# Seven products in place of eight in both halves of a feed-forward layer, with its row sums made on the chip from split rows

## The chip, the core and the metric

The kernel runs on one core of a Trainium2 chip. The metric is device time in microseconds (us). The kernel before took 1064.24 us (median of three runs, 1063.29 to 1064.33).

A core has five engines, each with a queue of its own that it works through in order: TensorE (PE; its weight loads are shown as PEld), VectorE (DVE), ScalarE (ACT), GpSimd (POOL) and SyncE (SP). SP computes nothing here; it issues most of the DMA transfers. POOL and ACT issue a few as well.

## The reference

All arrays are float32. S is 2048 rows, D is 576 columns, DFF is 4608.

```python
xn = layernorm(A_q)                                   # 2048 x 576, no scale or bias
k_shift = short causal convolution of A_k with shift_k (4 taps, per column)
kv = k_shift * A_v
y = long causal convolution of kv with ssm_k (2048 taps, per column, by FFT) + kv * ssm_D
out = A_q + xn * y + relu(xn @ B_w1) @ B_w2           # w1: 576 x 4608, w2: 4608 x 576
```

There are two independent pieces: the feed-forward layer (the two matrix products with the relu) and the long convolution, which the kernel does as a transform by matrix products. They meet in the last sum.

## The kernel before

**The arithmetic.** TensorE works on rounded float32, so each operand of the feed-forward layer is split into a high and a low part, and each product is three matmuls: high by high, high by low, low by high. A high part is made by an ACT copy, the low one by a subtraction: on POOL for weights (`split_lo`, line 428), on DVE for rows and for the hidden layer.

**The tiling.** The 2048 rows form four blocks of 512. The first half of the program works on two blocks, the second half on the other two. DFF is cut into 18 chunks of 256 columns (`NPAIR`), and both halves go through all 18. The program counts chunks 0 to 35: 0 to 17 in the first half, 18 to 35 in the second. A *visit* is one chunk with one block; there are 72, and each chunk is visited twice in a row, once with each block (`visits`, line 1125). In what follows "visit 8" is the ninth, which is the first with chunk 4.

**The first product, plain.** `mm1` (line 557) makes 128 hidden columns for 512 rows: 14 matmuls of 512 columns, 12 over four slices of 128 of D and two over the remaining 64, whose high and low part are stacked. A visit has two of them, 28 matmuls of 512. The rows are the transposed blocks `b1` and `b2` (slices 0, 2 and 1, 3) and `xr` (the remaining 64), each with high and low part.

**The first product by seven products.** `quad` (line 585) treats a visit as a 2 x 2 by 2 x 2 block product and makes seven products where eight would be plain. It needs sums of weight blocks (`sum_w` on POOL, line 486) and sums of row blocks: `t1`, which stands in the second half of `b1` in place of the plain rows, and `t2` to `t4` in a tile `t`. Each of the seven is six matmuls of 256 columns; the 64 remaining rows of D are added by four matmuls of 512. Between the products ACT copies two partial sums of 256 columns (lines 592, 593) and DVE adds two (597, 600). Before the change the whole first half uses `mm1` and the whole second half uses `quad`.

**The second product.** `unit` (line 612) takes 128 rows and 288 output columns through one or two chunks, six matmuls of 288 columns a chunk, and DVE adds the result to an accumulator (lines 634, 638). Units are queued by `phase` and taken by `fill` after each quarter of a visit, two units of one chunk or one of two chunks at a time.

**The convolution stream.** `conv` is a Python generator with four stages: `fk` (transform of the taps), `fx` (short convolution on DVE and transform of the rows), `fm` (product in the frequency domain) and `fo` (back transform, gate, sum). Each `yield` ends a step. `tick` (line 1077) counts the columns of feed-forward matmuls issued and takes the next step when a rate allows it; the rate comes from `SHARE`, the part of the feed-forward columns at which the stream is to end. A negative yield is a pause. The constants of `fk` and `fx` come by DMAs that POOL issues (`load_const`, line 665), three buffers deep. The instructions of each engine are finally ordered by a scheduler that goes by program order and by when it expects an operand to be ready.

**The rows of the second half.** `later_xT` (line 301) is a generator that makes, during the first half, the transposed and split rows of the blocks of the second half, with the row sums: it loads a block's four row tiles in two transfers of two tiles at a time, normalizes, stores them, loads them back in 32 x 32 blocks, turns them on DVE, sums and splits, and stores `b1` (with `t1` in it), `b2`, `t` and `xr` to DRAM (`kept`). Two tiles of 3072 floats a partition hold its work; they are those of `t`, which the first half does not use otherwise. `fetch` (line 415) loads everything back between the halves.

**Weights.** A chunk of `w1` lands in `both_w1`: in the first half alternately in its two halves of five slices; with the seven products one half takes the raw weights, the other the sums. A chunk of `w2` lands in two halves with a buffer each (tag `r2`, line 446), and the next load is queued right behind the split (`later_w2`). `opening` lists what the first visits do; `split_next` says when the weights of the next chunk are split.

## Time and profile before

| | us |
|---|---|
| median of three runs | 1064.24 |
| profiled execution, its own time | 1066.44 |
| profiled execution, span of the trace | 1064.6 |
| PE busy | 1051.3 |
| DVE busy | 740.6 |
| ACT busy | 550.9 |
| POOL busy | 399.1 |

The profiled execution took 1.84 us more than the span of its trace, and 2.2 us more than the median. Matmuls are pipelined: one of 288 columns is shown with 295 ns, though the next one starts 133 ns later. So the time of a matmul is read here from start to start in a row of them, not from its own duration. In the trace the first half's products carry the name `psh`, the second half's `psa` and `psb`; `pso` is the second product and `psf` the convolution.

### The profile page before, as it was taken

The page shows a single profiled execution, that of the slowest core. Times are in us where ns is not written, and L with a number is a line of the kernel's source. Part 1 is how long each engine was busy: PE and PEld are TensorE (multiplying, and loading weights), DVE is VectorE, ACT ScalarE, POOL GpSimd, SP SyncE. Part 2 cuts the span into 40 slices and gives each one's busy share as a digit, 9 for nine tenths or more (in the row PEclk, how much of TensorE's full clock was granted, in tenths as well). Part 3 has the DMA queues.
Part 4 walks back from the last instruction along what each step waited for, and adds up shares of the span by engine and source line. Part 5 has one row for each costly group of instructions (what it writes and reads, how often), then busy time and mean ns, then how long its engine had stood idle before and what let it go on. Part 6 is the DMA issues. An engine that isn't in the chain of part 4 may idle for free.

```text
span 1064.6 us, 19975 instructions
## 1 busy us (share of the span) xinstructions
PE 1051.3 (99%) x7153; PEld 989.4 (93%) x7153; DVE 740.6 (70%) x1312; ACT 550.9 (52%) x1201; POOL 399.1 (37%) x398
## 2 busy tenths in 40 slices
PE   8999999999999999999999999999999999999998
PEld 5889999998899999999999999999999999999997
DVE  4539778787776887752477788778787763666664
ACT  5226556434433434432467877777877753344341
POOL 4133333333133223342334334435244444444641
PEclk9999999999999999999999999999999999999999
DMA  9944867788656667754896566556556557667854
GB/s 229 204 100 133 227 174 203 207 242 228 192 157 185 161 177 221 237 160 165 275 264 193 157 181 181 174 182 188 160 154 204 166 168 219 213 206 228 276 183 111
DMA packets 156302, 204.44 MB, mean 192 GB/s; under 512 B 32845, under 2 KB 122703, under 8 KB 155180
## 3 DMA queue, kind: packets, MB, share of 16 engines
q1 hardware_dynamic: 143308, 189.00, 60.2%
q0 software_dynamic: 12576, 13.44, 5.6%
q8 instruction: 56, 0.92, 0.4%
q10 hardware_dynamic: 320, 0.74, 0.3%
q14 instruction: 42, 0.34, 0.1%
HBM read 133.92 MB, written 55.05 MB: 178 GB/s over the span
## 4 chain that ended last, share of the span: by engine, by line
PE 93%; DMA 3%; DVE 2%; ACT 1%; issue 1%; POOL 0%; SPq 0%; ACTq 0%; DVEq 0%
PE pso L629 41%; PE psh L566 21%; PE psb L542 13%; PE psf L904 7%; PE psa L542 6%; PE psf L684 3%; DMA acc<-in_x 1%; PE psf L1048 1%; PE psf L1050 1%; DMA both_w<-in_w 1%; DMA both<-in_v 1%; DMA xs<-both 0%; DVE both L821 0%; ACT hh L548 0%; DVE k L969 0%
## 5 line engine op out<-in xcount | busy, mean ns | idle before, releaser
L629 PE MATMUL pso<-w,hh 128*128 128x288 f32 x2304 | 469.2, 295 | 1.6 <-ACT w L528 0.8
L629 PEld LDWEIGHTS pso<-w,hh 128*128 128x128 f32 x2304 | 372.5, 188 | 9.0 <-ACT w L528 1.2
L629 PE MATMUL pso<-w,ll 128*128 128x288 f32 x1152 | 330.0, 295 | 0.0
L428 POOL TENSOR_TENSOR g<-both_w,g 128x256 fp32r<-128x256 f32 (+2 forms) x145 | 167.8, 1163 | 348.7 <-ACT g L466 294.4
L566 PE MATMUL psh<-b,g 128*128 128x512 f32 x864 | 218.7, 396 | 0.5 <-ACT b L223 0.2
L629 PEld LDWEIGHTS pso<-w,ll 128*128 128x128 f32 x1152 | 213.6, 188 | 1.0
L566 PEld LDWEIGHTS psh<-b,g 128*128 128x128 f32 x864 | 157.9, 189 | 31.1 <-DVE b L224 0.5
L638 DVE TENSOR_TENSOR acc<-pso,acc 128x288 f32<-128x288 f32 x232 | 101.8, 450 | 60.7 <-PE pso L629 59.1
L428 POOL TENSOR_TENSOR w<-r,w 128x576 fp32r<-128x576 f32 x72 | 113.8, 1580 | 57.4 <-ACT w L528 57.4
L548 ACT ACTIVATE hh<-psh 128x512 fp32r<-128x512 f32 x72 | 42.9, 597 | 148.6 <-PE psh L566 148.4
L549 DVE SCALAR_TENSOR_TENSOR ll<-psh,hh 128x512 fp32r<-128x512 f32 x72 | 49.3, 686 | 71.9 <-ACT hh L548 71.5
L542 PE MATMUL psb<-t,g 128*128 128x256 f32 x648 | 97.5, 281 | 0.3 <-DVE psa L597 0.3
L542 PEld LDWEIGHTS psb<-t,g 128*128 128x128 f32 x648 | 86.2, 188 | 2.4 <-DVE psb L600 1.1
L466 ACT ACTIVATE g<-both_w 128x256 fp32r<-128x256 f32 (+2 forms) x145 | 76.2, 542 | 10.7 <-PE psb L542 8.7
L495 POOL TENSOR_TENSOR both_w<-both_w 128x256 f32<-128x256 f32 x72 | 63.6, 902 | 28.9 <-DMA both_w<-in_w 27.5
L542 PE MATMUL psa<-b,g 128*128 128x256 f32 x432 | 63.3, 280 | 0.0
L542 PE MATMUL psb<-b,g 128*128 128x256 f32 x432 | 58.1, 281 | 0.0
L548 ACT ACTIVATE hh<-psa 128x512 fp32r<-128x512 f32 x36 | 21.5, 598 | 70.0 <-PE psa L542 69.8
L542 PEld LDWEIGHTS psa<-b,g 128*128 128x128 f32 x432 | 56.7, 188 | 0.0
L542 PEld LDWEIGHTS psb<-b,g 128*128 128x128 f32 x432 | 54.6, 188 | 0.0
L670 POOL DMA_DIRECT2D wx<-in_fwd x32 | 17.6, 549 | 98.5 <-PE psf L684 91.4
L634 DVE SCALAR_TENSOR_TENSOR acc<-pso,rstd,acc 128x288 f32<-128x288 f32 x72 | 36.5, 511 | 19.2 <-PE pso L629 18.5
(134 smaller groups left out, 1688.1 us busy)
## 6 DMA issues: line engine op xcount, KB each, us to landing
r<-in_w SPq DMA_DIRECT2D x72, 288.0 KB, 3.7
zy<-vo SPq DMA_DIRECT2D x64, 288.0 KB, 3.1
zo<-zy SPq DMA_DIRECT2D x32, 576.0 KB, 4.0
both_w<-in_w SPq DMA_DIRECT2D x35, 512.0 KB, 4.4
zk<-zk SPq DMA_DIRECT2D x64, 144.0 KB, 2.6
ztk<-zk SPq DMA_DIRECT2D x32, 288.0 KB, 3.3
ztx<-zx SPq DMA_DIRECT2D x32, 288.0 KB, 3.1
k<-k SPq DMA_DIRECT2D x64, 144.0 KB, 2.6
```

The lines of the kernel that those rows point to most:

```text
L428: return nc.gpsimd.tensor_tensor(dst, src, hi, OP.subtract)
L466: nc.scalar.activation(hi, src, AF.Copy)
L495: nc.gpsimd.tensor_tensor(dst, a, b, op)
L542: done["pe"] = nc.tensor.matmul(ps, a, m, start=start and i == 0, stop=i == len(seq) - 1, skip_group_check=not start)
L548: done["act"] = nc.scalar.activation(hh, ps, AF.Relu)
L549: lows.append(nc.vector.scalar_tensor_tensor(ll, ps, 0.0, hh, op0=OP.max, op1=OP.subtract))
L566: done["pe"] = nc.tensor.matmul(ps, a, m, start=i == 0, stop=i == len(seq) - 1)
L629: done["pe"] = nc.tensor.matmul(ps[:, :NH], a, m, start=c == 0, stop=c == len(seq) - 1)
L634: done["acc"] = nc.vector.scalar_tensor_tensor(acc[t][:, dc], ps[:, :NH], rstd[:, t:t + 1], acc[t][:, dc], op0=OP.mult, op1=OP.add)
L638: done["acc"] = nc.vector.tensor_tensor(acc[t][:, dc], ps[:, :NH], acc[t][:, dc], OP.add)
L684: nc.tensor.matmul(ps[:, :NH], w[:, n, :], stk, start=n == 0, stop=n == 1)
L904: nc.tensor.matmul(ps[:, :NH], a, m[:, cols], start=n == 0, stop=n == 2)
```

## The change

- `PLAIN = (4, 3)`: the first product is plain only for the first four chunks of the first half and the first three of the second. The other 14 and 15 chunks go by `quad`.
- `later_xT` no longer sums. It keeps plain split rows, and works in one row buffer of 576 floats (`spare`): one row tile at a time is loaded, normalized and stored, and pieces of 256 rows are loaded back, turned, split and stored. Its steps are taken after every quarter of a visit.
- `block_sums` makes `t2` to `t4` for a block on the chip from the split rows, in eight steps of DVE and ACT work, during the plain visits (visits 4 to 7, and 37 to 41). `first_sum` then writes `t1` over the second half of `b1`, when the last plain visit of that block is done: for one block at the end of visit 7 (41), for the other at the start of visit 8 (42), with two extra `fill()` behind it. `t` is neither stored to DRAM nor fetched.
- `w1` has one raw buffer from chunk 2 on. `w2` has one buffer in chunks 2 to 17, since the other one is the row buffer; `next_w2` queues its load a quarter of a visit later than before.
- The constants of `fk` have two buffers in place of three; the turned taps have two of their own in place of one shared with `quad`.
- `split_next` and `opening` follow: plain or summed weights by what the next chunk is.
- `SHARE` is 0.944 in place of 0.97, and a pause of the stream drops what credit it had.

The diff, cut to its core ("..." where lines are left out):

```diff
--- before.py
+++ after.py
@@ -33,6 +33,7 @@
 HALVES = 2
 HB = NB // HALVES
 HT = T // HALVES
+PLAIN = (4, 3)
-SHARE = 0.97
+SHARE = 0.944
-FFN_TOTAL = NPAIR * HB * (W_PLAIN + W_QUAD + 2 * 4 * W_UNIT)
-N_FLOATS = {"b1": 2048, "b2": 2048, "t": 3072, "xr": 512}
+FFN_TOTAL = HB * (sum(PLAIN) * W_PLAIN + (2 * NPAIR - sum(PLAIN)) * W_QUAD
+                  + 2 * NPAIR * 4 * W_UNIT)
+N_FLOATS = {"b1": 2048, "b2": 2048, "xr": 512}
+N_SUMS = 3072
...
-    nrm = dram.tile([HB, P, BT, D], F32, name="nrm")
+    nrm = dram.tile([HB, BT // 2, P, 2, D], F32, name="nrm")
...
-        hold, area = scratch(0, f"rows{b}"), scratch(1, f"area{b}")
...
+        row = spare
+        raw, out_ = row[:, :HR], row[:, HR:2 * HR]
+        both = row[:, :2 * HR].rearrange("p (m n) -> p m n", m=2)
+        for i in range(BT):
+            t = b * BT + i
+            move(row, x, t)
             yield
             yield
             with here():
+                stats(t, row)
+                inv_std(t, 1)
             yield
             with here():
+                normalized(row, row, t)
+            nc.sync.dma_start(nrm[s, i // 2, :, i % 2], row)
+            yield
+        for c in range(5):
+            n = min(P, D - c * P)
+            for r in range(2):
+                rows = slice(r * HR, (r + 1) * HR)
+                src = nrm[s, r].rearrange("(e r) i d -> r i e d", e=4)
+                to = raw[:n].rearrange("p (i e d) -> p i e d", e=4, d=Q)
+                for q in range(n // Q):
+                    nc.sync.dma_start(to[q * Q:(q + 1) * Q],
+                                      src[..., c * P + q * Q:c * P + (q + 1) * Q])
+                yield
+                yield
+                hi = raw[:n].bitcast(F32R)
+                with here():
+                    nc.vector.transpose(out_[:n], raw[:n])
+                    nc.scalar.activation(hi, out_[:n], AF.Copy)
+                yield
+                with here():
+                    nc.vector.tensor_tensor(out_[:n].bitcast(F32R), out_[:n], hi, OP.subtract)
+                if c < 4:
+                    kept_ = kept["b2" if c % 2 else "b1"][s].rearrange("p (m k n) -> p m k n",
+                                                                      m=2, k=2)
+                    nc.sync.dma_start(kept_[:, :, c // 2, rows], both)
+                else:
+                    for m in range(2):
+                        nc.sync.dma_start(kept["xr"][s][64 * m:64 * m + 64, rows], both[:64, m])
+                yield
+
+    def block_sums(s):
+
+        b1, b2 = f32(ops[s, "b1"]), f32(ops[s, "b2"])
+        t = operand(s, "t")
+        tt = nc.vector.tensor_tensor
+        v, w = sum_v, xp.tile([P, NH], F32, tag="m5", name=f"sum{s}", bufs=1)[:, :HR]
+
+        def both(b, kp, r):
+            return [b[:, m, kp, r * HR:(r + 1) * HR] for m in range(2)]
+
+        def high(i, kp, src):
+            nc.scalar.activation(t[:, i, 0, kp], src, AF.Copy)
+
+        def low(i, kp, src):
+            tt(t[:, i, 1, kp], src, t[:, i, 0, kp], OP.subtract)
+
+        for kp in range(2):
+            (h11, l11), (h12, l12) = (both(b1, kp, r) for r in range(2))
+            (h21, l21), (h22, l22) = (both(b2, kp, r) for r in range(2))
+            with here():
+                tt(v, h22, h12, OP.subtract)
+                tt(v, v, l22, OP.add)
+                tt(v, v, l12, OP.subtract)
+                high(1, kp, v)
...
+    def first_sum(s):
+
+        b1 = ops[s, "b1"]
+        tt = nc.vector.tensor_tensor
+        w = xp.tile([P, NH], F32, tag="m5", name=f"first{s}", bufs=1)[:, :HR]
+        for kp, v in enumerate((sum_v, w)):
+            (h11, l11), (h12, l12) = ([f32(b1)[:, m, kp, r * HR:(r + 1) * HR] for m in range(2)]
+                                      for r in range(2))
+            tt(v, h12, h11, OP.subtract)
+            tt(v, v, l12, OP.add)
+            tt(v, v, l11, OP.subtract)
+            nc.scalar.activation(b1[:, 0, kp, HR:], v, AF.Copy)
+        for kp, v in enumerate((sum_v, w)):
+            tt(b1[:, 1, kp, HR:], v, b1[:, 0, kp, HR:], OP.subtract)
...
-                t = t.rearrange("p a b c -> p (a b c)" if name != "t"
-                                else "p k a b c -> p (k a b c)")
+                t = t.rearrange("p a b c -> p (a b c)")
             nc.sync.dma_start(f32(t), kept[name][s])
...
     both_w1 = wp.tile([P, 10, FC], F32, name="both_w1", bufs=1)
+    raw_w2 = wp.tile([P, FT * NH], F32, name="raw_w2", bufs=1)
+    spare = wp.tile([P, FT * NH], F32, name="spare", bufs=1)
+    sum_v = both_w1[:, 9]
+
+    def plain(n):
+        return n % NPAIR < PLAIN[n // NPAIR]
 
     def load_w1(n):
         f0 = (n % NPAIR) * FC
-        r1 = both_w1[:, 5:] if n < NPAIR and n % 2 else both_w1
+        r1 = both_w1[:, 5:] if n == 1 else both_w1
...
     def load_w2(n, h):
         f0 = (n % NPAIR) * FC
-        r2 = wp.tile([P, FT, NH], F32, tag="r2", name=f"r2_{n}_{h}", bufs=2)
+        r2 = spare if h and not 2 <= n < NPAIR else raw_w2
+        r2 = r2.rearrange("p (j d) -> p j d", j=FT)
         nc.sync.dma_start(r2, w2[f0:f0 + FC, h * NH:(h + 1) * NH]
                           .rearrange("(j p) d -> p j d", p=P))
         raw_w[n, h] = r2
...
-    def load_const(pool, src, name, late=False):
-        w = pool.tile([P, 2, P], F32R, tag="wt", name=name, bufs=3)
+    def load_const(pool, src, name, bufs=3, late=False):
+        w = pool.tile([P, 2, P], F32R, tag="wt", name=name, bufs=bufs)
...
                 ws = {}
-                for n in range(3):
-                    ws[n] = load_const(fp, fwd[n // U][:, n % U], f"wk{n}", late=True)
+                for n in range(2):
+                    ws[n] = load_const(fp, fwd[n // U][:, n % U], f"wk{n}", 2, late=True)
...
-                    pool, tag = (xp, "m5") if i % 2 else (fp, "tr")
-                    tr = turned_[i] = pool.tile([P, NH], F32, tag=tag, name=f"tr{t2}", bufs=1)
+                    tr = turned_[i] = fp.tile([P, NH], F32, tag="tr", name=f"tr{t2}", bufs=2)
...
-                    if n + 3 < len(order):
-                        ws[n + 3] = load_const(fp, fwd[(n + 3) // U][:, (n + 3) % U], f"wk{n + 3}")
+                    if n + 2 < len(order):
+                        ws[n + 2] = load_const(fp, fwd[(n + 2) // U][:, (n + 2) % U],
+                                               f"wk{n + 2}", 2)
...
         if c < 0:
             clock["until"] = clock["ffn"] - c
+            clock["conv"] = min(clock["conv"], 0.0)
         else:
             clock["conv"] -= c
...
+    def next_w2(n, h):
+        if n == 0 or NPAIR <= n < HALVES * NPAIR - 1:
             load_w2(n + 1, h)
-
-    opening = {(0, 1): [(later_w2, 0, 0)], (0, 3): [(later_w2, 0, 1)],
-               (1, 1): [(later_w2, 1, 0)], (1, 2): [(load_w1, 2), (load_w1, 3)], (1, 3): [(later_w2, 1, 1)],
+        elif n < NPAIR - 1 or n == NPAIR - 1 and not h:
+            if not h and n > 1:
+                load_w2(n, 1)
+            elif (n == 1) != bool(h):
+                load_w2(n + 1, 0)
+        elif n == NPAIR - 1:
+            for h_ in range(2):
+                load_w2(n + 1, h_)
...
+    def all_sums(q):
+        return (step_ for q_ in (q, q + 1) for step_ in block_sums(visits[q_][1]))
+
+    lasts = [2 * (half * NPAIR + PLAIN[half] - 1) for half in range(HALVES)]
+    begins = [4, 2 * NPAIR + 1]
+    sums_ = [all_sums(q) for q in lasts]
...
-        parts = quad(n, s, q % 2) if half else None
+        if q - 2 in lasts:
+            first_sum(s)
+            fill()
+            fill()
+        parts = None if plain(n) else quad(n, s, q % 2)
...
-            if half:
+                if st == 2 and n > 2:
+                    next_w2(n, second)
+            if not plain(n):
                 tick(W_STAGE[st])
-            if q > 3 and (st % 2 or st == 2 and q % 2):
+            if begins[half] <= q <= lasts[half] + 1:
+                next(sums_[half], None)
+            if q - 1 == lasts[half] and st == 3:
+                for _ in sums_[half]:
+                    pass
+                first_sum(visits[q - 1][1])
+            if q > 3:
                 next(ahead, None)
             fill()
         if m == NPAIR - 1 and not half:
...
-            fetch(s, ("t",))
```

More of the change, by code (lines that the diff above doesn't have):

```diff
@@ L367, in later_xT @@
-        for c in range(2):
-            for q in (0, 2):
-                load(c, (q, q + 1))
-                yield
-        yield
-        for kp in range(2):
-            hi, lo = (b2[:, m].bitcast(F32R) for m in range(2))
-            with here():
-                e0 = turn_over(2 * kp)
-            b11, b12 = e0[:, r12[0]], e0[:, r12[1]]
+        row = spare
[4 more added lines that the diff above has]
+            move(row, x, t)
+            yield
@@ L1131, in split_next @@
     def split_next(n, second, st):
-        if n + 1 < NPAIR:
+        if n + 1 == HALVES * NPAIR:
+            return
+        if plain(n + 1) and plain(n):
             if not second:
@@ L1140, in split_next @@
                 split_rest(n + 1)
-                if n + 3 <= NPAIR:
-                    load_w1(n + 3)
-        elif n + 1 == NPAIR:
+                load_w1(n + 2)
+        elif plain(n + 1):
+            if second:
+                if st < 2:
+                    split_plain(n + 1, st)
+                elif st == 2:
+                    split_rest(n + 1)
+                else:
+                    load_w1(n + 2)
+        elif plain(n):
             if not second:
@@ L1153, in split_next @@
                 load_w1(n + 2)
-        elif n + 1 < HALVES * NPAIR:
-            if second:
-                split_group(n + 1, st)
-                if st == 3 and n + 2 < HALVES * NPAIR:
-                    load_w1(n + 2)
-            else:
-                sum_w(n + 1, st)
+        elif second:
+            split_group(n + 1, st)
+            if st == 3 and n + 2 < HALVES * NPAIR:
+                load_w1(n + 2)
+        else:
+            sum_w(n + 1, st)
     def later_w2(n, h):
@@ L1196, in h3_ffn_kernel @@
                     later_w2(n, second)
-            if half:
+                if st == 2 and n > 2:
+                    next_w2(n, second)
+            if not plain(n):
                 tick(W_STAGE[st])
-            if q > 3 and (st % 2 or st == 2 and q % 2):
+            if begins[half] <= q <= lasts[half] + 1:
[5 more added lines that the diff above has]
+            if q > 3:
                 next(ahead, None)
```

102 lines of the change are left out of this document (17 added, 85 removed).

## The prediction

> **What bounds the kernel now.** I read the page first, then the table of windows, then the timeline of PE.
>
> ```profile
> span 1064.6 us, 19975 instructions
> ...
> PE 1051.3 (99%) x7153; PEld 989.4 (93%) x7153; DVE 740.6 (70%) x1312; ACT 550.9 (52%) x1201; POOL 399.1 (37%) x398
> ```
>
> PE is busy in 1051.3 of 1064.6 us. Since matmuls overlap, "busy" does not yet say that it works at its best pace. The windows say more (time, busy time and instruction count of each engine, granted clock, DMA share, GB/s):
>
> ```profile
> core 0: us, PE busy (x) PEld busy (x) DVE busy (x) ACT busy (x) POOL busy (x), PEclk, DMA share, GB/s
> 240.00:280.00 40.00, 36.37 (x210) 32.69 (x209) 32.07 (x48) 17.82 (x36) 10.69 (x12) 0.96 0.80 215
> 280.00:500.00 220.00, 220.00 (x1320) 199.88 (x1320) 151.45 (x243) 84.62 (x170) 68.29 (x66) 1.00 0.63 183
> 560.00:700.00 140.00, 139.26 (x1055) 136.23 (x1055) 109.26 (x190) 104.37 (x233) 57.20 (x48) 1.00 0.60 176
> 700.00:850.00 150.00, 149.98 (x1147) 147.83 (x1146) 117.89 (x202) 113.75 (x255) 65.64 (x55) 1.00 0.58 175
> ```
>
> In both halves (280 to 500 plain, 560 to 850 with seven products) PE has no idle time to speak of, at the full granted clock. DVE is at 69% in the first and 78% in the others. Only 240 to 280 stands out: PE idle for 3.6 us, and the clock at 0.96 of full. Outside that place a change moves the time if it moves the number or the length of the matmuls. So I need their spacing, from the timeline of PE (start, duration, what, count), first a plain product, then pieces of a seven-product visit:
>
> ```profile
> 386.79 2.95 PE L566 MATMUL psh<-b,g 128*128 128x512 f32 x12
> 389.58 0.63 PE L566 MATMUL psh<-xr,g 128*128 128x512 f32 x2
> 390.05 0.43 PE L629 MATMUL pso<-w,hh 128*128 128x288 f32 x2
> ```
>
> ```profile
> 743.05 0.87 PE L542 MATMUL psb<-t,g 128*128 128x256 f32 x6
> 743.76 0.87 PE L542 MATMUL psa<-b,g 128*128 128x256 f32 x6
> 744.47 0.63 PE L542 MATMUL psa<-xr,g 128*128 128x512 f32 x2
> 744.94 0.30 PE L904 MATMUL psf<-hix,m_sb 128*128 128x288 f32 x1
> ```
>
> From start to start, 14 matmuls of 512 take 390.05 - 386.79 = 3.26 us. Six of 256 take 0.71 us, and the two of 512 behind them 0.47 us.
>
> **Part 1: visits that go from plain to seven products.** Before, 36 of 72 visits use `quad`; after, 2 x 14 + 2 x 15 = 58. So 22 more do (28 gained in the first half, 6 lost in the second). A plain visit is 2 x 3.26 = 6.52 us of PE; one by seven products is 7 x 0.71 + 2 x 0.47 = 5.91 us. That is 0.61 us a visit, and 22 x 0.61 = **13.4 us less**. Nothing else on PE changes in number.
>
> A rule speaks against this part. The Trainium skill (Perfetto Trace Analysis, section Identifying the Most-Contended Engine) says that matmul busy time misleads and that the busy share of weight loads tells how near TensorE is to its limit. By that, more loads would cost more: a visit goes from 28 loads to 46. In the rows, the loads are busy in 199.88 of 220 us in the plain window and in 147.83 of 150 with seven products, so by this reading the second half is bound by loads. But there six matmuls of 256, each with its own load, follow each other in 0.71 us, or 118 ns each, against 3.26 / 14 = 233 ns for twice the columns. The loads are in that spacing already. I take the spacing.
>
> What the 22 visits add elsewhere lies beside PE:
>
> ```profile
> L600 DVE TENSOR_TENSOR psb<-psb,m 128x256 f32<-128x256 f32 x36 | 15.4, 427 | 14.6 <-PE psb L542 14.4
> ...
> L593 ACT ACTIVATE psa<-psb 128x256 f32<-128x256 f32 x36 | 13.7, 379 | 0.7 <-DVE ll L549 0.6
> ```
>
> DVE gets two such additions a visit, 22 x 2 x 0.427 = 18.8 us, ACT 22 x 2 x 0.38 = 16.7 us. Inside a visit DVE's addition stands between two products. In the second half units and stream steps cover it, and the windows show no idle PE there, so I cost it at nothing; without that cover it would be some 0.4 us twice a visit, up to 19 us.
>
> **Part 2: the row sums on the chip.**
>
> ```profile
> L404 DVE TENSOR_TENSOR area<-area 128x256 f32<-128x256 f32 x4 | 6.4, 1590 | 0.0
> ...
> L388 DVE TENSOR_TENSOR area<-rows 128x256 f32<-128x256 f32 x4 | 1.7, 414 | 0.0
> ```
>
> These are the same subtraction, at 414 ns undisturbed and at 1590 ns where it met other work. `block_sums` has 20 such DVE operations for a block and `first_sum` 8, so four blocks cost 112 operations, 46 us at the short price. `later_xT` loses 50 of its own and gets 20 new splits, so DVE has 82 more, 34 us at the short price: with part 1, 740.6 + 18.8 + 34 = 793 us of some 1052, or 75%. DVE has that room on average. What may show is the place where a sum gates a product. At visit 7 the first block's `t1` is made a visit ahead and costs nothing. At visits 8 and 42 the other block's `t1` gates the first product at once. Its chain is 8 x 0.414 + 2 x 0.38 = 4.1 us at the short price, 13.5 us at the long one. The cover is two extra fills, 24 matmuls of 288, which the chain of the end gives as:
>
> ```profile
> 397.19 3.19 PE pso L629 x24
> ```
>
> Exposed are 0 to 10 us at each place. Most of the chain reads only what is ready early, so the short price is nearer: 4.1 - 3.2 = 0.9 us twice, **2 us more** with rounding for the units that those visits then lack.
>
> **Part 3: the stall at 252 to 274.** This is the one place where the rest of the change can win. The chain of waits:
>
> ```profile
> 252.47 6.90 DMA both<-in_v
> ...
> 259.44 4.43 DMA both_w<-in_w
> ```
>
> and what SP issued around it:
>
> ```profile
> 251.91 0.47 SPq L160 DMA_DIRECT2D rows<-in_x  x1
> 252.47 1.21 SPq L160 DMA_DIRECT2D both<-in_v  x2
> 253.73 1.23 SPq L160 DMA_DIRECT2D rows<-in_x  x2
> ```
>
> The rows of `v` for the stream took 6.9 us to land, beside the issues of the next block's row tiles and a weight load; DVE, then the copies to `xs`, then PE waited. The loss is 3.6 us of idle PE and (1 - 0.96) x 36.4 = 1.5 us of slow clock, 5.1 us. After the change a block's rows come one tile at a time, spread over four visits, so this crowd does not form. Next late would be the stream's own loads of `k` and `v`. Against that, `later_xT` now queues a row load behind the store of the row before it (same buffer), and each load of a piece behind the store of the piece before; SP waits there, and stores of `zx`, loads of `k` and `v`, the copies to `xs` and weight loads wait behind it, and the stream's matmuls for those. I let 3 of the 5.1 us stay somewhere in `fx`: **2.1 us less**, with 5.1 less to 5 more as bounds.
>
> **Part 4: two buffers for the constants of `fk`.** The view of the tile `wk`:
>
> ```profile
> L684 PE MATMUL psf<-ks,wk x128: 290/295/302, 82.4 to 205.5; 128*128 128x288 f32 x128
> ...
> DMA to landing us min/median/max: 2.3/3.1/7.2
> ```
>
> 32 units stand in 123 us, 3.97 us apart. A buffer comes free at a unit's last matmul, 0.3 us after its start. With two, the load must land before the next unit but one: 1.5 x 3.97 - 0.3 = 5.7 us later, 5.3 us if the stream runs some 5% denser between pauses (the new rate). It needs 0.3 + 3.1 = 3.4 us in the median, 7.5 us at worst. So most loads are in time, and a late one costs PE up to 2.2 us. POOL also waits at such an issue, with weight sums and splits queued behind it, and those are due a visit later. At one load in ten late by 1 us, and a bit for the irregular spacing: **1.5 us more**; bounds 0 and 30 x 2.2.
>
> **Edits at nothing.** One raw buffer for `w1` and `w2` in the first half: a load must land within a visit of some 13 us; hidden, and if not, one landing. `t` no longer written or fetched: transfers beside PE. The later end of the stream: its last matmul starts 17 us before the last of the second product now (1041.6 against 1059.0 in the rows below), a reserve I expect to shrink but not to go.
>
> ```profile
> L1050 PE MATMUL psf<-zo,wi x64: 289/294/303, 886.5 to 1041.6; 128*128 128x288 f32 x64
> ```
>
> ```profile
> L629 PE MATMUL pso<-w,ll x1152: 288/295/442, 25.4 to 1059.0; 128*128 128x288 f32 x192
> ```
>
> **The sum.** -13.4 + 2.0 - 2.1 + 1.5 = -12.0 us. On the span that gives 1064.6 - 12.0 = 1052.6 us. The profiled execution's own time, 1066.44 us, would become 1054.4. The median of the runs is 2.2 us below it, so I predict 1064.24 - 12.0 = **1052 us**.
>
> **Rivals.**
>
> *A. DVE and POOL meet more often, and DVE becomes late in `fx`.* POOL gets, for each of 11 more summed chunks, four sums and two more splits:
>
> ```profile
> L428 POOL TENSOR_TENSOR g<-both_w,g 128x256 fp32r<-128x256 f32 (+2 forms) x145 | 167.8, 1163 | 348.7 <-ACT g L466 294.4 <-PE pso L629 29.2 <-PE psf L904 15.4
> ...
> L495 POOL TENSOR_TENSOR both_w<-both_w 128x256 f32<-128x256 f32 x72 | 63.6, 902 | 28.9 <-DMA both_w<-in_w 27.5
> ```
>
> 4 x 0.90 + 2 x 1.16 = 5.9 us a chunk. A visit is 6.52 us of the first product and 48 x 3.19 / 24 = 6.4 us of the second, with stream matmuls between, so 280 to 500 holds some 16 visits or eight chunks, and 47 us of this. If DVE were blocked for all of it, DVE would need 151 + 16 x 0.85 + 47 = 212 us in a stretch that shrinks to 210; if for half, 188 us. So DVE comes near its limit at most, and the price is lateness at the stream's operations, like the stall above: two more of 5 us, 1062 us. For it speaks this pair from the timelines of POOL and DVE:
>
> ```profile
> 264.93 1.44 POOL L428 TENSOR_TENSOR w<-r,w 128x576 fp32r<-128x576 f32 x1
> ```
>
> ```profile
> 264.54 2.45 DVE L821 TENSOR_TENSOR both<-both 128x576 f32<-128x576 f32 x1
> 266.91 0.75 DVE L815 TENSOR_TENSOR both<-both 128x576 f32<-128x576 f32 x1
> ```
>
> The DVE operation took 2.45 us where one of the same shape took 0.75, and it ended 0.6 us after POOL's. The Trainium skill (SBUF — State Buffer, section SBUF: two separate sides) calls the port pair of the two engines an exclusive lock, held for a whole instruction; by that rule the blocking is nearer the full 47 us, and this pair agrees. Against it: from 560 to 850 POOL is busy for 122.84 of 290 us, more than this, and PE did not idle. Chance 0.14.
>
> *B. The stall goes and nothing takes its place*, at visits 8 and 42 too: 1064.2 - 13.4 - 5.1 = 1046 us. Chance 0.12.
>
> *C. Slower: the constants of `fk` come late every time.* Place: 82 to 205, 30 loads. It decides when the mean lateness passes 12.0 / 30 + 0.05 = 0.45 us a load, so when the mean way from free buffer to landing is over 5.7 us. At 1 us each, in place of my 1.5 us in all, it gives 1052 + 28 = 1080 us. The median landing of 3.1 us speaks against it. Chance 0.06.
>
> *D. Loads, not columns, set the pace in the first half too*, as the rule of part 1 would have it: 22 x 18 more loads at their 188 ns would be 74 us more, 1138 us. The spacing of 118 ns excludes nearly all of it. Chance 0.01.
>
> *E. The gain is eaten within 0.2%* by several of these without one that decides: 1063 us. Chance 0.05.
>
> **How the numbers follow.** The forecast has the remaining 0.62. A measurement of this kernel can tell 0.2%, some 2 us, from no change. Forecast and B are faster; of A, whose times lie between 1057 and 1064, I count 0.11 as faster and 0.03 as same. So faster 0.85, same 0.08, slower 0.07 (C and D). The range goes from 1046 (B) to 1062 (A).
>
> **What would show it.** `quad` products from about 120 us on, in rows of six at 0.71 us; 58 x 42 matmuls of 256 columns. PE's idle time between 200 and 500 below 4 us, if part 3 holds. Gaps ahead of `psf<-ks,wk` under 2 us in all, or rival C. DVE below 90% in `fx`, or rival A. I am wrong in the main term if the first-half products come at more than 0.71 us for six, or if PE stands idle for over 10 us in the first half.

## The result, and the profile after

| | before | after |
|---|---|---|
| median of the runs, us | 1064.28 (4 runs, 1063.29 to 1066.21) | 1113.58 (4 runs, 1109.38 to 1116.74) |
| profiled execution, us | 1066.44 | 1115.53 |
| its span, us, and granted clock | 1064.6, 0.998 | 1113.8, 0.985 |

The kernel after is slower: the ratio is 1.046, with a 95% interval from 1.042 to 1.050, or 49.3 us. The forecast was 1052 us.

The page of the kernel after has these lines in answer to those shown of before; the last is the first row of the chain that ended last, by engine:

```profile
span 1113.8 us, 21280 instructions
...
PE 1061.6 (95%) x7549; PEld 1010.9 (91%) x7549; DVE 795.8 (71%) x1475; ACT 581.0 (52%) x1299; POOL 449.6 (40%) x464
...
PE 63%; DVE 18%; DMA 11%; issue 3%; ACT 2%; SPq 2%; POOL 1%; DVEq 0%; ACTq 0%; POOLq 0%
```

PE was idle for 13.3 us before and for 1113.8 - 1061.6 = 52.2 us now. The chain to the end, which stays on PE when PE sets the pace, now runs through DVE for 18% and through transfers for 11% of the span. DVE's busy time, 795.8 us, is about the 793 us of the forecast's sum; yet DVE is where PE waits. The table of windows says in which stretches:

```profile
core 0: us, PE busy (x) PEld busy (x) DVE busy (x) ACT busy (x) POOL busy (x), PEclk, DMA share, GB/s
82.00:100.00 18.00, 16.14 (x95) 13.98 (x94) 17.46 (x40) 7.29 (x18) 6.51 (x8) 1.00 0.39 113
100.00:120.00 20.00, 17.98 (x100) 16.08 (x98) 17.99 (x39) 11.51 (x28) 8.71 (x10) 0.91 0.48 139
120.00:140.00 20.00, 13.56 (x80) 11.15 (x80) 19.46 (x44) 8.96 (x23) 6.73 (x10) 0.98 0.50 141
200.00:500.00 300.00, 274.52 (x2008) 265.33 (x2007) 218.12 (x366) 125.47 (x275) 144.15 (x143) 0.97 0.58 160
700.00:850.00 150.00, 150.00 (x1150) 148.03 (x1149) 109.27 (x203) 114.56 (x258) 58.62 (x55) 1.00 0.61 182
```

The same view of the kernel before:

```profile
82.00:100.00 18.00, 18.00 (x109) 16.32 (x109) 17.33 (x41) 10.02 (x23) 6.28 (x8) 1.00 0.51 137
100.00:120.00 20.00, 20.00 (x129) 18.55 (x128) 16.53 (x32) 13.34 (x30) 7.62 (x10) 1.00 0.72 213
120.00:140.00 20.00, 20.00 (x122) 18.12 (x121) 14.64 (x24) 11.02 (x26) 7.04 (x9) 1.00 0.76 194
...
200.00:500.00 300.00, 296.37 (x1766) 268.80 (x1766) 213.79 (x343) 116.81 (x235) 92.06 (x90) 0.99 0.68 195
```

The second half (700 to 850) is as it was. From 82 to 140, where the row sums now run, DVE is busy in 54.9 of 58 us (95%, before 84%) and PE loses 10.3 us. These visits are still plain: the first matmul of a seven-product visit starts at 141.1 us. Yet before, DVE was at 17.33 of 18 us in the first of these stretches, and PE lost nothing. From 200 to 500 DVE has hardly more to do than before, 73% of the time, and PE still loses 25.5 us, with a lower clock besides.

Did the products themselves cost what was forecast? The timeline of PE in the first half, away from any wait:

```profile
326.01 0.86 PE L539 MATMUL psa<-b,g 128*128 128x256 f32 x6
326.71 0.86 PE L539 MATMUL psb<-t,g 128*128 128x256 f32 x6
327.41 0.42 PE L626 MATMUL pso<-w,hh 128*128 128x288 f32 x2
```

Six matmuls in 0.70 us: the main term is there. Take for each shape the undisturbed spacing of the prediction's rows (118 ns for 256 columns, 133 for 288, 233 for 512) and add up by how much the start-to-start times of all matmuls exceed it: some 14 us before, some 77 us after. That is 63 us more of waiting and slow clock against 13.4 us less of work, and 63 - 13.4 = 49.6 us is close to the measured difference. The 63 us lie so: 21 from 50 to 150 us, most of it ahead of the first seven-product visit, 4 to 200, 32 from 200 to 500, where the visits are by seven products, and 6 behind that.

What PE waited for, of the kernel after (total, times, longest, in us):

```profile
PE psb L539 <- DVE psa L594: 8.0, 5, 4.2
PE psf L681 <- DVE ks L674: 7.6, 9, 1.5
PE psb L539 <- DVE psb L597: 6.4, 5, 2.9
PE psf L681 <- DMA xs<-both: 4.1, 2, 3.5
PE pso L626 <- DVE acc L631: 3.7, 5, 1.2
PE pso L626 <- DVE acc L635: 3.3, 3, 2.1
PE psf L681 <- DMA wk<-in_fwd: 3.0, 3, 1.2
```

Before, the largest such row was 3.6 us. Two of the three largest are the additions in the middle of a `quad` (L594, L597), which the forecast costed at nothing. One of these waits, in the timelines of PE, DVE, POOL and SP:

```profile
472.65 1.26 SPq L330 DMA_DIRECT2D spare<-nrm  x2
...
474.87 0.86 PE L539 MATMUL psb<-t,g 128*128 128x256 f32 x6
...
475.69 0.44 DVE L336 STREAM_TRANSPOSE spare<-spare 64x256 f32<-64x256 f32 x1 [3.26 <-DMA spare<-nrm]
476.06 0.71 DVE L832 TENSOR_TENSOR both<-both 128x576 fp32r<-128x576 f32 x1
476.80 0.76 DVE L812 TENSOR_TENSOR both<-both 128x576 f32<-128x576 f32 x1
...
477.59 1.96 DVE L813 TENSOR_TENSOR both<-both 128x576 f32<-128x576 f32 x2
...
478.09 4.05 POOL L492 TENSOR_TENSOR both_w<-both_w 128x256 f32<-128x256 f32 x4 [2.74 <-DMA both_w<-in_w]
...
479.47 0.42 DVE L594 TENSOR_TENSOR psa<-psb,m 128x256 f32<-128x256 f32 x1
...
479.95 1.25 PE L539 MATMUL psb<-t,g 128*128 128x256 f32 x6 [4.21 <-DVE psa L594]
480.99 1.48 PE L539 MATMUL psa<-b,g 128*128 128x256 f32 x6
482.27 1.05 PE L539 MATMUL psa<-xr,g 128*128 128x512 f32 x2
483.13 1.21 PE L539 MATMUL psb<-t,g 128*128 128x256 f32 x6
```

Read it from the top. A piece of a row is loaded into the row buffer. DVE's turn of it (L336) stands at the head of DVE's queue and waits for the landing, 3.26 us. Behind it stand four steps of the stream, and behind those the addition (L594) for which PE has been waiting since 475.7. One operation that waits for a transfer has thus moved its wait to everything behind it on its engine. This is not the only such place: from 141 to 560 us PE is idle 20 times for over 0.4 us, 27.9 us in all, and in 12 of them, 17.8 us, DVE had waited for a transfer of `later_xT` while PE was idle or in the 6 us before. After the stall, six matmuls take 1.04 us instead of 0.70 (479.95 to 480.99): the stall is paid for once more in a slow clock.

### The profile page after: what moved, and what is told of

Same layout as the page of the kernel before. It is cut to its first block, busy times and chain, and to the rows that moved or that the text cites. A ratio compares the mean times of both kernels' runs of the same rounds, so it can differ in the third digit from the quotient of the medians.

```text
span 1113.8 us, 21280 instructions
## 1 busy us (share of the span) xinstructions
PE 1061.6 (95%) x7549; PEld 1010.9 (91%) x7549; DVE 795.8 (71%) x1475; ACT 581.0 (52%) x1299; POOL 449.6 (40%) x464
## 4 chain that ended last, share of the span: by engine, by line
PE 63%; DVE 18%; DMA 11%; issue 3%; ACT 2%; SPq 2%; POOL 1%; DVEq 0%; ACTq 0%; POOLq 0%
PE pso L626 26%; PE psb L539 15%; PE psa L539 7%; PE psf L901 6%; PE psh L563 4%; DVE both L813 2%; PE psf L681 2%; DVE both L812 2%; DMA spare<-nrm 2%; DVE ks L674 2%; DVE acc L635 1%; DMA kept_b<-spare 1%; DVE ll L546 1%; SPq L330 1%; PE psw L1106 1%
## 5 line engine op out<-in xcount | busy, mean ns | idle before, releaser
L418 POOL TENSOR_TENSOR g<-both_w,g 128x512 fp32r<-128x512 f32 (+2 forms) x167 | 190.6, 1150 | 389.7 <-ACT g L463 238.5
L539 PE MATMUL psb<-t,g 128*128 128x256 f32 x1044 | 156.8, 284 | 14.7 <-DVE psa L594 8.0
L539 PEld LDWEIGHTS psb<-t,g 128*128 128x128 f32 x1044 | 140.4, 191 | 19.0 <-DVE psa L594 9.9
L539 PE MATMUL psa<-b,g 128*128 128x256 f32 x696 | 104.5, 284 | 0.0
L418 POOL TENSOR_TENSOR w<-raw_w,w 128x576 fp32r<-128x576 f32 x52 | 80.8, 1553 | 54.2 <-ACT w L525 54.1
L463 ACT ACTIVATE g<-both_w 128x512 fp32r<-128x512 f32 (+2 forms) x167 | 86.4, 539 | 14.2 <-PE psb L539 11.8
L563 PE MATMUL psh<-b,g 128*128 128x512 f32 x336 | 85.2, 396 | 0.5 <-ACT b L226 0.2
L563 PEld LDWEIGHTS psh<-b,g 128*128 128x128 f32 x336 | 61.1, 188 | 12.8 <-DVE b L227 0.5
L546 DVE SCALAR_TENSOR_TENSOR ll<-psa,hh 128x512 fp32r<-128x512 f32 x58 | 39.7, 685 | 28.2 <-ACT hh L545 28.2
L546 DVE SCALAR_TENSOR_TENSOR ll<-psb,hh 128x512 fp32r<-128x512 f32 x58 | 39.7, 685 | 13.2 <-ACT hh L545 12.8
```

Source lines behind the costliest of these rows:

```text
L418: return nc.gpsimd.tensor_tensor(dst, src, hi, OP.subtract)
L463: nc.scalar.activation(hi, src, AF.Copy)
L539: done["pe"] = nc.tensor.matmul(ps, a, m, start=start and i == 0, stop=i == len(seq) - 1, skip_group_check=not start)
L546: lows.append(nc.vector.scalar_tensor_tensor(ll, ps, 0.0, hh, op0=OP.max, op1=OP.subtract))
L563: done["pe"] = nc.tensor.matmul(ps, a, m, start=i == 0, stop=i == len(seq) - 1)
```

## The experiments

Each edited kernel below was timed once, beside the kernel before on the same chip in the same job, unless a ratio with its interval is given. The four runs of the kernel after lie between 1109 and 1117 us, and 17 runs of the kernel before in one job between 1062.7 and 1070.3, so a gain under some 8 us is not told from none. "Gain" is against the kernel after, by the differences to before: 49.3 us less the run's own.

The first four runs had three theories: the waits of the single row buffer (theory 1), DVE filled by the row sums (theory 2), or seven-product visits that stall by themselves in the first half (theory 3).

### e1: no loads of the pieces

```diff
-                for q in range(n // Q):
-                    nc.sync.dma_start(to[q * Q:(q + 1) * Q], ...)
```

> The changed kernel without the loads of the row pieces in later_xT (the turns, splits and stores stay and work on whatever the buffer holds, so the rows of the second half are left out). Theory 1, the single row buffer: SP queues each piece load behind the store of the piece before, VectorE waits at the turn with everything behind it, and TensorE waits for VectorE; then VectorE's 24 us of waits for these loads between 200 and 500 us go, and some 25 to 30 us of the time: about 1085 us. Theory 2, VectorE is full while the row sums are made (82 to 140 us): no change between 200 and 500, about 1110 us. Theory 3, the seven products in the first half stall of themselves, since each visit needs VectorE twice between its products: within 8 us of 1113.

1105.97 against 1066.86 us: 39.1 us slower than before, a gain of 10. From 200 to 500 PE was still idle for 20.2 us. The wait shown above is one part, not the whole.

### e2: the first half plain again, without its row sums, all else as changed

```diff
-PLAIN = (4, 3)
+PLAIN = (18, 3)
...
-    sums_ = [all_sums(q) for q in lasts]
+    sums_ = [iter(()), all_sums(lasts[1])]
```

> The changed kernel with the first half plain throughout and no row sums there; later_xT, the buffers and the second half as changed. 28 visits go back to plain products, 17 us more of TensorE. Theory 1: the stalls between 200 and 500 stay (some 35 us with the slow clock), those of 82 to 140 go: 1113 + 17 - 20 = 1110 us. Theory 3: with plain products the lateness is absorbed, TensorE idles as little as in the kernel before: 1064 + 4 for six plain visits in the second half = 1068 to 1075 us.

1070.03 against 1066.86: 3.2 us slower, of which six visits that are plain in the second half where before has seven products make 6 x 0.61 = 3.7. That is where theory 3 put it; e10 and e11 below show that the visits by seven products don't stall by themselves. So `later_xT` with its single buffer, two buffers for `wk` and the single raw buffers cost nothing that shows as long as the first half is plain and makes no row sums. Its windows:

```profile
200.00:500.00 300.00, 299.66 (x1794) 271.67 (x1793) 212.42 (x350) 117.32 (x240) 91.20 (x93) 1.00 0.66 183
```

DVE hardly waits for row pieces here. Its waits for these loads, first in the kernel after, then in e2 from 200 to 500 (total, times, longest, in us):

```profile
DVE spare L336 <- DMA spare<-nrm: 25.1, 10, 5.9
```

```profile
DVE spare L336 <- DMA spare<-nrm: 0.8, 1, 0.8
```

With the waits for whole rows, and those at a turn that the view puts down to another transfer, DVE waits 35.9 us for `later_xT` in the kernel after from 60 to 520 us and 3.8 us in e2. So e2 does not say what a plain visit does with a late turn, and why the turns come late when the visits are by seven products is not shown by any run.

### e3: no row sums

```diff
-                tt(v, h22, h12, OP.subtract)
...
+                    high(i, kp, a)
+                    nc.scalar.activation(t[:, i, 1, kp], c_, AF.Copy)
```

> The changed kernel with VectorE's part of the row sums left out: t2 to t4 and t1 are filled by ScalarE copies of single blocks, so the products are not the reference's. Theory 2: the 10 us of idle and the slow clock behind it between 82 and 200 us go, 20 us less: about 1093 us, and the stretch from 200 on is as before. Theories 1 and 3: less than 6 us.

1094.79 against 1066.86: 27.9 us slower, a gain of 21. PE ran in 55.4 of the 58 us from 82 to 140 (47.7 in the kernel after). Theory 2 holds for that stretch, whose visits are plain in the kernel after; but its windows from 200 on show that the rest stays:

```profile
200.00:500.00 300.00, 276.48 (x2046) 267.73 (x2044) 221.59 (x367) 128.87 (x282) 147.00 (x146) 0.98 0.60 165
```

### e4: a third place for the raw piece

```diff
-        raw, out_ = row[:, :HR], row[:, HR:2 * HR]
+        raw, hi_, out_ = sum_v, row[:, :HR], row[:, HR:2 * HR]
...
+                if i + 1 < len(pieces):
+                    load(*pieces[i + 1])
```

> The changed kernel with a third place of 256 floats for later_xT (the raw piece lands in the tile of the row sums, which is free then), and each piece load issued right behind the turn before it, so that no load waits for a store. Nothing is left out. Theory 1: SP's waits for kept stores and VectorE's for piece loads go, 25 to 30 us less: about 1085 us. Theory 3: within 8 us of 1113 us.

1116.96 against 1066.86: 50.1 us slower, no gain. DVE's wait for the pieces (25.1 us over the span in the kernel after) is gone from its list of waits; its waits for whole rows rose from 3.9 to 12.6 us, 4.4 us at the turns are now for stores, and PE's waits for `psa` rose from 8.0 to 15.8. Theory 1 alone falls: DVE waits less for transfers (17.0 us in place of 35.9), and PE loses as much.

The next four asked which property of the seven-product visits meets the lateness.

### e5: the two additions as copies on ScalarE

```diff
-        nc.vector.tensor_tensor(pa[:, other], pb[:, first], m5, OP.add)
+        nc.scalar.activation(pa[:, other], pb[:, first], AF.Copy)
...
```

> The changed kernel, but in the first half the two additions between the products of a visit are ScalarE copies of one summand (the sum is left out, TensorE now waits for ScalarE there). Theory A: TensorE loses its time because VectorE's addition, which the next product needs at once, stands in VectorE's queue behind the long operations of the stream and of later_xT; then most of the 36 us lost between 200 and 500 us go, 25 us less or more, some 25 us over the kernel before. Theory C: VectorE is late in general, and TensorE will wait for other results of it (accumulators, copies to xs): less than 8 us gained.

1105.97 against 1069.28: 36.7 us slower, a gain of 13. The waits for `psa` and `psb` went, and others grew. In its list of waits (L687 is L681 of the kernel after):

```profile
PE psf L687 <- DVE ks L680: 11.0, 13, 2.5
PE psb L539 <- DVE ll L546: 6.5, 5, 2.7
```

PE is caught at the next place where it needs DVE: the stream's operands, or the low half of the hidden layer that frees the bank.

### e6: no weight sums on POOL

```diff
+        if n < NPAIR:
+            return
```

> The changed kernel without GpSimd's sums of weight blocks in the first half (the products take what lies there). Theory B: VectorE is late because GpSimd's 44 more sums there block its two-input operations, which then take up to twice and three times as long: 15 us less or more. Theory A: the queue alone does it, 3 to 8 us less.

1110.51 against 1069.28: 41.2 us slower, a gain of 8, and 1110.51 lies among the runs of the kernel after, so it is not told from none. That POOL's weight sums of the first half, 56 operations, stand in DVE's way is a small part at most: from 200 to 500 the stream's two-input operations of 128 x 576 on DVE take 835 ns in the mean before, 994 after and still 981 here. POOL's additional splits stay in e6.

### e7: e3 and e5 together

> The additions by ScalarE copies as above, and the row sums by ScalarE copies as in the run without sums. If theory A and the full VectorE of 82 to 140 us are the two causes, and independent, their gains add up: 20 + 25 us, some 4 us over the kernel before or less, with TensorE idle under 15 us. Theory C: more than 20 us over the kernel before.

1088.98 against 1069.28: 19.7 us slower, a gain of 30, less than 21 + 13. From 200 to 500 the matmuls still exceed their spacing by some 25 us.

### e8: the stream held behind the additions

```diff
-        nc.vector.tensor_tensor(pa[:, other], pb[:, first], m5, OP.add)
+        done["acc"] = nc.vector.tensor_tensor(pa[:, other], pb[:, first], m5, OP.add)
...
```

> Nothing is left out: the stream's steps are ordered behind the latest of a visit's two additions, as they are now behind the latest accumulation. Theory A: additions wait for fewer stream operations, 8 to 20 us less. If VectorE cannot spare the time in which it then waits for TensorE, the stream's own results come late and nothing is won, or up to 10 us are lost.

1104.95 against 1069.28: 35.7 us slower, a gain of 14 with nothing left out. The order in DVE's queue seems to matter (this run is 4.4 us under the fastest of the kernel after), and as in e5 the waits move: those for `wk` rise from 3.0 to 10.3 us.

Then: does the lateness come from the stream, or from `later_xT`?

### e9: the stream only after the first half

```diff
-START = 24000
+START = 960000
```

> The changed kernel with the convolution stream held back until the first half is done (START at 960000 columns; nothing is left out, and the second half becomes long). Read is the first half alone, from 150 to 430 us. Theory D: a visit by seven products goes back and forth between TensorE and VectorE or ScalarE in each quarter, in the same two banks, and bears a lateness of VectorE of 1 or 2 us, where a plain visit bears several; the stream's long operations and its waits make that lateness. Then TensorE idles for under 4 us in that stretch. Theory E: the seven products stall by themselves in the first half (one raw buffer for each weight, GpSimd's sums): 20 us or more of idle stay.

The whole run, 1318.91 us, says nothing, since the stream now follows alone at the end. What was wanted is the first half without a stream:

```profile
150.00:430.00 280.00, 264.94 (x2002) 259.44 (x2001) 110.58 (x241) 81.01 (x178) 116.21 (x117) 0.99 0.29 79
```

DVE is busy for 39% of the time, and PE is still idle for 15.1 us, between what the two theories said, all of it ahead of the addition of L594. So neither a full DVE nor the stream is needed for this loss. How much the stream adds can't be read here: without its matmuls the visits follow each other faster, and the row transfers have less time. The chain of waits in one of the places (start, us, what):

```profile
379.37 3.31 DMA kept_b<-spare
...
382.70 0.56 SPq L330
...
383.96 0.61 SPq L436
...
385.81 0.60 SPq L330
...
386.46 3.08 DMA spare<-nrm
...
389.62 0.09 DVE spare L336
...
389.98 0.41 DVE psa L594
...
390.44 1.65 PE psb L539 x6
```

The store of one piece, then the loads of the next, since both use the one row buffer, with weight loads between them in SP's order; then the turn on DVE, and behind it the addition, and behind that PE. 10.6 us go from the store's start to the addition.

### e10 and e11: no rows ahead

e10 leaves `later_xT` out; e11 has the edits of e3 and e5 as well.

```diff
-    ahead = (step for b_ in range(HB, NB) for step in later_xT(b_))
+    ahead = iter(())
```

> The changed kernel without later_xT (the second half works on the first half's rows again, stored once). Theory D: VectorE's 30 us of waits for row tiles and pieces go, and its other work there; of the 36 us lost between 200 and 500 us 12 to 20 go, and some of the 20 us before: about 25 us over the kernel before. Theory E: little, under 8 us.

> Without later_xT, with the additions and the row sums by ScalarE copies. Theory D: nearly all sources of lateness that the change brought are gone and the stream alone remains; TensorE loses under 12 us in the first 600 us beyond its start, and the time is 5 us under to 5 us over the kernel before. Theory E: 15 us over or more.

e10: 1075.29 against 1065.02, 10.3 us slower, a gain of 39. e11: 1059.09 against 1065.02, 5.9 us faster than before. With `later_xT`, the additions and the row sums off DVE, some of the saving appears. e11's windows:

```profile
200.00:500.00 300.00, 295.69 (x2244) 289.49 (x2243) 212.25 (x280) 147.51 (x325) 155.81 (x150) 1.00 0.57 160
```

### e12: before, its row loads spread

This asks what the stall at 252 to 274 of the kernel before was worth, and whether spreading the loads makes before better.

```diff
-        for _ in range(4):
+            yield
             yield
```

> The kernel before, with one edit: the two loads of row tiles at the head of later_xT stand two steps apart in place of back to back. If the crowd of loads makes the stall at 252 to 274 us, it goes, 3 to 5 us less, about 0.4%. If not, no difference.

1065.53 us (12 runs) against 1065.02 us (17 runs), ratio 1.0003 with an interval from 0.9992 to 1.0015: no difference. The matmuls of its profiled execution exceed their spacing by 1.9 us at this stall, those of before by 5.6 us; the median doesn't show it, and the other executions have no trace that could say whether they stall there.

### e13 and e14: the same delay in plain and in seven-product visits

Eight small in-place DVE operations per visit of the first half, added to e2 (all visits plain, e13) and to e11 (seven products, e14).

```diff
+            if q > 3 and not half and st == 1:
+                with here():
+                    for _ in range(8):
+                        nc.vector.tensor_scalar(ident, ident, 1.0, None, op0=OP.mult)
```

> The run with a plain first half, with eight small VectorE operations (128 x 128, in place, times one; some 1.6 us together) put into each first-half visit from the fifth on. Theory F: a plain visit bears this lateness: TensorE loses under 6 us in all against the run without it, so about 3 to 9 us over the kernel before. If VectorE's time as such is what counts, 32 x 1.6 = 50 us more.

> The same delay in the run without later_xT, with additions and row sums by ScalarE copies (6 us under the kernel before without the delay). Theory F: a visit by seven products does not bear it, though less other work is on VectorE here than in the plain run: 0.4 to 1.6 us for each of 28 visits, 11 to 45 us more, 5 to 40 us over the kernel before. Without such a difference: under 6 us more, as in the plain run.

e13: 1076.78 against 1065.33, 11.5 us slower than before and 8.3 more than e2. e14: 1084.57 against 1065.33, 19.2 us slower and 25.2 more than e11. The windows of e13:

```profile
200.00:500.00 300.00, 296.75 (x1761) 267.95 (x1760) 254.61 (x518) 116.40 (x238) 89.56 (x91) 0.99 0.65 180
```

and those of e14:

```profile
200.00:500.00 300.00, 283.72 (x2119) 274.54 (x2119) 252.22 (x442) 140.93 (x309) 154.33 (x149) 0.99 0.51 141
```

DVE is at 85% and 84%. PE is idle for 3.3 us in the plain visits and for 16.3 us in the others. The same delay costs three times as much in the one as in the other (25.2 against 8.3 us), so at these shares it is not DVE's busy time alone that decides. What makes the difference is not shown. In e14 the additions are on ACT, and PE's largest waits from 200 to 500 are for accumulators (8.6 us) and for the low half of the hidden layer (3.6 us); POOL and ACT have more to do than in e13 as well.

### e15 and e16: the two parts of `later_xT` alone

e15 keeps its DVE and ACT operations and leaves all its transfers out; e16 keeps the transfers and leaves the operations out.

```diff
-            move(row, x, t)
...
-            nc.sync.dma_start(nrm[s, i // 2, :, i % 2], row)
```

```diff
-                stats(t, row)
-                inv_std(t, 1)
...
-                    nc.vector.transpose(out_[:n], raw[:n])
```

> The changed kernel with later_xT's operations of VectorE and ScalarE, but none of its transfers (the operations work on what lies in the buffer; the second half gets the first half's rows). If the waits for transfers make the lateness: near the run without later_xT, 5 to 18 us over the kernel before. If the work in VectorE's queue makes it: 35 us over or more.

> The changed kernel with later_xT's transfers, but none of its operations of VectorE and ScalarE (mean and deviation of the second half's rows are those of the first half's). VectorE has nothing to wait for here. If the turn's wait is the link, this is near the run without later_xT, 5 to 18 us over the kernel before; if SP's crowd of transfers delays the stream and the weights by itself, 25 us over or more.

e15: 1105.99 against 1065.33, a gain of 9. e16: 1122.57 against 1065.33, 8 us slower still than the kernel after. Each part alone is nearly enough for the loss, so they don't add up, and their shares can't be read from these. e16 shows a second road by which lateness reaches PE. From 94.5 to 98.2 us SP issues four loads of row pieces with two weight loads between them; the weights land at 101.2, POOL waits for them, and the constant of `fk` is issued by POOL behind that. Its timeline of POOL, and then that of PE (L671 is L681 of the kernel after):

```profile
101.28 2.08 POOL L482 TENSOR_TENSOR both_w<-both_w 128x256 f32<-128x256 f32 x3 [9.13 <-DMA both_w<-in_w]
103.30 0.55 POOL L657 DMA_DIRECT2D wk<-in_fwd  x1
```

```profile
106.42 0.82 PE L671 MATMUL psf<-ks,wk 128*128 128x288 f32 x2 [8.43 <-DMA wk<-in_fwd]
```

## Why the prediction was wrong, point by point

**The main term was right.** 22 more visits by seven products were to save 13.4 us. The spacing is the forecast one (0.70 us for six), and 2436 = 58 x 42 matmuls of 256 columns stand in the trace. In e11, where most of the waits are taken away, the matmuls exceed their spacing by some 7 us more than before, and 13.4 - 7 = 6 us is what e11 is faster. Rival D took the busy share of weight loads for the measure of how near TensorE is to its limit (the Trainium skill, Perfetto Trace Analysis, section Identifying the Most-Contended Engine); it is not borne out here: with 265.33 us of loads in 300 the six still take 0.70 us.

The excess of the matmuls over their spacing, counted as above, shows by stretches what each edit takes away (us; excesses of 5 ns or less are left out):

| | 50 to 150 | 200 to 500 |
|---|---|---|
| before | 0.6 | 6.0 |
| after | 21.6 | 38.5 |
| e2, first half plain, no sums there | 0.6 | 1.6 |
| e3, no row sums | 4.8 | 34.0 |
| e5, additions on ACT | 21.0 | 26.0 |
| e10, no `later_xT` | 11.7 | 11.7 |
| e11, all three of e3, e5 and e10 | 1.9 | 6.3 |

**The step that failed is in part 1:** "In the second half units and stream steps cover it, and the windows show no idle PE there, so I cost it at nothing". The cover was read off a half in which, before the change, neither `later_xT` nor the row sums nor `fk` and `fx` are in DVE's queue. From 200 to 500 the loss is 32 us in place of nothing. PE waited 14.4 us in ten places for the additions themselves (8.0 + 6.4), the longest 4.21 us at 475, since it waits for all that stands ahead of an addition in DVE's queue; the text's 0.4 us twice a visit priced the addition alone. Its sum for lost cover, up to 19 us, would have held for the additions (e5 gains 13), but not for the other results of DVE and the transfers that PE is caught at when the additions are moved. The largest source in this stretch is `later_xT`: without it 11.7 of the 38.5 us stay (e10). e9 shows that the stream isn't needed for a loss, and e13 and e14 that at an equal share of DVE a first half by seven products loses more to the same delay than a plain one.

**Part 2's "DVE has that room on average" failed as well,** and this is a loss of its own: 21 us from 50 to 150, of which 17 lie ahead of 141 us, in plain visits. The sums were put at 2 us, by two exposed chains; without them the kernel after gains 21 (e3), and 4.8 of the 21.6 us of that stretch stay. The forecast's sum of DVE's time came true, and in the 58 us where the sums are made DVE was at 95%; there PE waited mostly for the stream's operands (`ks`) and for accumulators; additions of seven-product visits there were none yet. That stretch had 84% before the change, by the windows of before, which the forecast did not read. `later_xT` has a share in it: without it 11.7 us stay.

**Part 3:** 2.1 us were to be won at the stall. e2 has no stall there, and e12 shows that its loss in before can't be measured in the median. The text did name the new order's risk, loads queued behind stores and other work behind those; but its bound, 5 us more, is far under what `later_xT` costs in seven-product visits.

**Part 4:** the constants of `fk` were put at 1.5 us; PE waited for them for 3.0 us. The gaps ahead of `psf<-ks,wk` were to be under 2 us "or rival C"; they are more, but the larger part is `ks` on DVE (7.6 us), so rival C is not what happened.

**The rivals.** A had the direction, DVE late in `fx`, but of its mechanism, POOL in DVE's way, the weight sums gave 8 us at most (e6), and it priced two late places; from 60 to 560 us there are 35 at which the next matmul starts over 0.4 us late. It rested on DVE's share of the time, as the forecast did, and so did the sign "DVE below 90% in `fx`": DVE was at 73% from 200 to 500 and late all the same. The sign that did speak was PE's idle time, over 4 us between 200 and 500 and over 10 us in the first half. The text took the latter for a fault of the main term; it was one of the cover and of the sums.

**Of the 63 us:** 39 are idle time of PE (52.2 - 13.3). Most of the rest is the slow clock after the gaps: 0.985 against 0.998 of full over the span is (1 - 0.985) x 1061.6 - (1 - 0.998) x 1051.3 = 14 us. Of the 10 us left some 7 belong to the gaps: a matmul is shown as busy past the start of the next one, so each gap hides some 0.17 us of its wait (after, 54 gaps show 45.5 us of idle time and exceed the spacing by 54.6; before, 10 gaps show 6.2 and exceed it by 7.9).

**What stays open.** How the loss divides between the work and the transfers of `later_xT` (e15, e16); why its turns come late with seven-product visits and not with plain ones (e2); and which hand-over inside the visit matters most: with the additions moved off DVE, PE is caught at others (e5, e14). Each edit also lets the scheduler order the queues anew, and no run holds that order fixed. Why the second half bears a DVE at 73% with the same visits is only argued, from what DVE's queue does not hold from 700 to 850: `later_xT`, row sums, `fk` and `fx`. No version was found that does the whole work and is faster than before; e11, the only one ahead of before, leaves out work that the result needs.

## What to carry to other kernels

When an operation is added between two products, ask how long before PE needs its result it can start, and then list everything that can stand ahead of it in its engine's queue in that very stretch, above all operations that wait for a transfer: their whole wait can become its price, also where the engine's busy share is low, as in e9. A cover seen in another stage counts only if the same streams are in the queue there. And read the windows of the stretch into which work is moved, not at the engine's average over the span.

## What the runs showed of the hardware

The clock after a gap: the windows of the kernel after behind the wait of 4.21 us.

```profile
480.00:482.00 2.00, 2.00 (x11) 2.00 (x12) 1.18 (x2) 0.00 (x0) 1.92 (x3) 0.61 0.70 196
482.00:484.00 2.00, 2.00 (x10) 1.81 (x9) 0.01 (x1) 0.64 (x2) 0.14 (x1) 0.53 0.51 148
484.00:486.00 2.00, 2.00 (x16) 1.91 (x16) 1.54 (x3) 1.43 (x4) 0.55 (x1) 1.00 0.16 39
```

For some 4 us the granted clock is about half, then it is full again. The products in that time lost 1.6 us, so this gap cost 4.21 + 1.6 us. That agrees with what the Trainium skill says (TensorE: Matmul & The Clock Gate, section Part 1: The HAM clock gate (the "warmup" mystery)), that an idle array falls to half its rate and needs some 3.4 us of work to come back. The page speaks of an idle window of the same 3.4 us; here a gap of 2.1 us that ended at 299 us was already followed by 1.6 us of such loss, one of 1.6 us that ended at 396 us by 0.1.
